# Later rows of x and the map of k: from TensorE transposes to VectorE's 32x32 blocks with quarters moved by DMA, with a newly sought order

## The chip, the cores and the metric

The kernel runs on one core of one Trainium2 chip. The metric is the device time of one execution in microseconds; the kernel before takes 705.9 us, the median of 3 runs (704.93 to 706.68). The profile is of one execution, taken by the hardware profiler.

## The reference

The input is x (2048 rows of 512, float32). It is normalised by rows, and two branches are computed from it and joined:

```
xn = layernorm(x)                                  # rows: (x - mean) / sqrt(var + 1e-5)
q, k, v = xn @ wq, xn @ wk, xn @ wv                # 32 heads of 16
for each of 4 segments s of 512 rows:
    p     = softmax(q_s k_s^T / 4 + causal mask)   # per head
    a_dot = p v_s
    a_mem = (phi(q_s) M) / (phi(q_s) z + 1e-6)     # phi(t) = t + 1 if t > 0 else exp(t)
    o_s   = g a_mem + (1 - g) a_dot                # g = sigmoid(beta) per head
    M += phi(k_s)^T v_s ; z += sum of phi(k_s)
h   = relu(xn @ w1) @ w2                           # 512 -> 1792 -> 512
out = x + (o @ wo) * silu(h)
```

The matmuls have to be more exact than one pass gives, so each operand is split into a high and a low part (xh and xl, wh and wl, and so on), and a product takes three matmuls: high by high, low by high, high by low.

## The kernel before

**Tiling.** The four segments follow one another, 512 rows each. Within a segment the heads are taken in four groups of eight, so there are 16 groups n, and each group has two halves u of four heads. TensorE contracts over the partition axis, so every product that contracts over the 512 columns of x needs x with its columns on partitions: the tiles `xh` and `xl` (128 partitions, 4 column blocks, 512 rows) are the two parts of x turned. They are read by the projections (`proj`, `vproj`) and the first MLP layer (`w1chain`).

**How x is turned before.** `lnload` (L623) loads the four tiles of 128 rows of a segment into buffers of the ring `io`; `lnstat` (L667) takes mean and variance on VectorE (L634), finds 1/sqrt by four Newton steps on GpSimd (L684 to L687), and normalises the tiles in place, two on VectorE and two on GpSimd (L698). `ln` (L709) then turns each tile with four TensorE transposes (L725) into a bank of PSUM, from which ScalarE writes the high part (L732) and VectorE the low one (L733). The first segment has a path of its own, `lnstat0`, in the opening.

**How k is turned before.** For the memory M the product contracts over rows, so phi(k) of a group, tile `pk` (128 head columns on partitions, 512 rows), has to be turned too. `memory` (L1144) does it with four TensorE transposes (L1154) into a bank, which ScalarE copies to `pkT` (L1159). `memory2` (L1166) then multiplies `pkT` by v (L1182). This is done for the 12 groups of the first three segments.

**The rest, where the prediction speaks of it.** Most products run in two lanes, `lanes` (L798): a contraction of 128 is cut into a lower half (L829) and an upper half (L838), each of 64 rows of the array, and the upper half of an earlier product runs beside the lower half of a later one; a half without a partner runs alone. Between them stand the row maxima, q k^T on TensorE (L1225) and a VectorE maximum for each (L1231, `CUSTOM_DVE` in the profile, `ISA` in the order); the scores again for the exponentials (L1277, then L1294 and L1288 on ScalarE); p v (L1323); the memory's numerator and denominator (L1112, L1113). Weights come by DMA into `io` (L516); ScalarE splits off the high part (L527) and GpSimd the low one (L528). q and k go through DRAM (`sdq`, `sdk`, L1064, L1065) to be stacked (L1199), the row maxima too (L1251, L1252). `output` and `silu` (L918, L969, L973) end a segment.

**What sets the order.** Everything is issued by a planner in the kernel's source, class `Sched` (L94): each operation has an assumed length and a due time, and a list scheduler places it on its engine's queue. All DMAs but three go through SyncE's queue, which takes them in order. `search` (L274) repeats the planning twelve times with due times fed back, and then tries random moves, one per number in `STEPS` (L48). The result is one fixed order for every engine. The loop over t in `emit` has 179 steps; group n has its projections at step 10n - 17, `memory(n)` at 10n - 9 and `memory2(n)` at 10n.

## Time and profile before

| | |
|---|---|
| runs | 706.68, 704.93, 705.9 us; median 705.9 |
| span of the profiled execution, first to last instruction | 703.0 us |
| TensorE matmul (PE) / weight load (PEld) | 99% / 79% busy |
| VectorE (DVE), ScalarE (ACT), GpSimd (POOL) | 63%, 59%, 64% busy |
| granted TensorE clock | 1.000 |
| DMA | 125,490 packets, 139.88 MB, 199 GB/s over the span |

The page gives the profiled execution's span alone and no time of its own beside it. Busy shares are means over the whole span. A row of a group reads: line, engine, operation, out<-in, shapes, number | busy us, mean ns of one | idle time before it and what ended that. A piece of the chain that ended last reads: start, length, what. The matmuls on TensorE overlap, so the sum of their lengths is more than the time that they take; the chain's pieces do not overlap. SPq is SyncE's queue of DMA issues.

### The profile page before, as it was taken

How to read it: one execution, taken by the hardware profiler on the slowest of the kernel's cores; microseconds unless marked ns; L12 is line 12 of the kernel's file. 1: busy time of each engine (PE TensorE's matmuls, PEld its weight loads, DVE VectorE, ACT ScalarE, POOL GpSimd, SP SyncE). 2: the span in 40 equal slices, each digit the busy share in tenths (PEclk: the TensorE clock that was granted, in tenths of full speed). 3: DMA queues.
4: the chain of work that ended last, by engine and by line, in shares of the span. 5: the costliest groups of instructions: out<-in, count | busy, mean ns of one | idle time of the engine just before them, and what ended most of it. 6: DMA issues, size and time to landing. Idle time of an engine off the chain costs nothing.

```text
span 703.0 us, 18592 instructions
## 1 busy us (share of the span) xinstructions
PE 696.8 (99%) x6818; PEld 552.8 (79%) x6818; DVE 444.1 (63%) x1398; ACT 413.1 (59%) x633; POOL 448.6 (64%) x567
## 2 busy tenths in 40 slices
PE   8999999999999999999999999999999999999997
PEld 7989787777877688787788878777887977777776
DVE  4357777676968673666683766466577647566427
ACT  5544656666857583475674667446466546665642
POOL 5643754737649476676594947757675667675854
PEclk9999999999999999999999999999999999999999
DMA  5787556656676479475566658837575767763514
GB/s 187 218 271 238 167 173 217 197 171 207 213 256 187 153 245 297 129 232 183 151 218 227 192 169 284 256 118 258 160 245 183 254 200 232 240 220 90 168 22 129
DMA packets 125490, 139.88 MB, mean 199 GB/s; under 512 B 24712, under 2 KB 70024, under 8 KB 125400
## 3 DMA queue, kind: packets, MB, share of 16 engines
q1 hardware_dynamic: 125192, 138.50, 61.7%
q8 instruction: 54, 0.88, 0.5%
q14 instruction: 36, 0.29, 0.1%
q10 hardware_dynamic: 208, 0.20, 0.1%
HBM read 99.01 MB, written 34.93 MB: 191 GB/s over the span
## 4 chain that ended last, share of the span: by engine, by line
PE 97%; DMA 1%; DVE 0%; SPq 0%; issue 0%; ACT 0%; DVEq 0%
PE ps L829 56%; PE ps L838 11%; PE ps L1323 10%; PE pt L1277 6%; PE ps L1225 6%; PE pt L1112 2%; PE ps L725 1%; PE ps L1154 1%; PE ps L789 1%; PE ps L787 1%; PE ps L788 1%; DMA io<-in_A_wv_dram 1%; DMA nn<-F 1%; PE ps L1182 1%; PE pt L787 0%
## 5 line engine op out<-in xcount | busy, mean ns | idle before, releaser
L1231 DVE CUSTOM_DVE_ANT_0 none<-ps,causal 128x256 bf16<-128x256 f32 (+3 forms) x512 | 250.8, 490 | 117.7 <-PE ps L1225 80.2
L528 POOL TENSOR_TENSOR wl<-io,wh 128x512 fp32r<-128x512 f32 x176 | 225.9, 1295 | 77.2 <-ACT wh L527 68.9
L1294 ACT ACTIVATE P<-pt 128x1024 f32<-128x1024 f32 x128 | 131.2, 1025 | 69.5 <-PE pt L1277 66.7
L829 PE MATMUL ps<-xh,wh 64*128 64x512 f32 x352 | 139.5, 396 | 0.0
L838 PE MATMUL ps<-xl,wh 64*128 64x512 f32 x352 | 139.1, 395 | 0.0
L838 PE MATMUL ps<-xh,wl 64*128 64x512 f32 x352 | 136.9, 389 | 0.0
L838 PE MATMUL ps<-xh,wh 64*128 64x512 f32 x352 | 136.8, 389 | 0.0
L829 PE MATMUL ps<-xl,wh 64*128 64x512 f32 x352 | 136.6, 388 | 0.0
L829 PE MATMUL ps<-xh,wl 64*128 64x512 f32 x352 | 136.6, 388 | 0.0
L527 ACT ACTIVATE wh<-io 128x512 fp32r<-128x512 f32 x176 | 108.1, 629 | 25.6 <-PE ps L838 8.7
L1284 POOL TENSOR_SCALAR_AFFINE_SELECT P<-P 128x512 f32<-128x512 f32 x128 | 80.4, 640 | 61.5 <-ACT P L1294 46.4
L838 PE MATMUL ps<-wl,hh 64*128 64x512 f32 x224 | 89.4, 399 | 0.0
L829 PE MATMUL ps<-wh,hh 64*128 64x512 f32 x224 | 89.0, 397 | 0.0
L838 PE MATMUL ps<-wh,hl 64*128 64x512 f32 x224 | 87.2, 389 | 0.0
L838 PE MATMUL ps<-wh,hh 64*128 64x512 f32 x224 | 87.1, 389 | 0.0
L829 PE MATMUL ps<-wh,hl 64*128 64x512 f32 x224 | 86.9, 388 | 0.0
L829 PE MATMUL ps<-wl,hh 64*128 64x512 f32 x224 | 86.9, 388 | 0.0
L1323 PE MATMUL ps<-P,vt 128*17 128x512 f32 (+3 forms) x1024 | 75.1, 434 | 0.0
L829 PEld LDWEIGHTS ps<-xh,wh 64*128 64x128 f32 x352 | 64.9, 185 | 10.5 <-issue 2.8
L829 PEld LDWEIGHTS ps<-xh,wl 64*128 64x128 f32 x352 | 64.8, 184 | 10.4
L1225 PE MATMUL ps<-ks,qs 64*128 64x256 f32 (+3 forms) x512 | 70.4, 324 | 0.3 <-DVE F L1061 0.3
L829 PEld LDWEIGHTS ps<-xl,wh 64*128 64x128 f32 x352 | 65.0, 185 | 6.7
(172 smaller groups left out, 1724.3 us busy)
## 6 DMA issues: line engine op xcount, KB each, us to landing
io<-in_B_w_dram SPq DMA_DIRECT2D x112, 256.0 KB
qs<-sdq SPq DMA_DIRECT2D x32, 512.0 KB
ks<-sdk SPq DMA_DIRECT2D x32, 512.0 KB
sdq<-F SPq DMA_DIRECT2D x16, 512.0 KB
sdk<-F SPq DMA_DIRECT2D x16, 512.0 KB
io<-in_A_x_dram SPq DMA_DIRECT2D x28, 256.0 KB
io<-in_A_wv_dram SPq DMA_DIRECT2D x16, 256.0 KB
io<-in_A_wq_dram SPq DMA_DIRECT2D x16, 256.0 KB
```

The lines of the kernel that those rows point to most:

```text
L527: act(512, [rk], [hk], lambda: ACT.activation(h, raw, AF.Copy), 7.0 + nsplit if early else 6.0)
L528: pool(512, [rk, hk], [lk], lambda: POOL.tensor_tensor(l, raw, r32(h), op=OP.subtract), 8.5 + 1.3 * nsplit if early else 25.4)
L725: PE.transpose(pt[:, 128 * c:128 * c + 128], xt[:, 128 * c:128 * c + 128], ident)
L829: i = PE.matmul(m[0], m[2][0][LO], m[2][1][LO], start=m[4], stop=False)
L838: PE.matmul(h[0], h[2][0][HI], h[2][1][HI], start=False, stop=h[5] is not None)
L1112: PE.matmul(pn[r:r + 64], MZ[r:r + 64, r:r + 64], f[r:r + 64], start=True, stop=True)
L1225: PE.matmul(two[a][0][:, o:o + w], qs[r, p, w - 128:w], ks[r, p, :w], start=True, stop=True)
L1231: dve(w + 40 + TTR, [pk, "causal"], [f"{dk}.{p}{a}{j}"], lambda p=p, j=j, o=o, w=w, a=a, pS=pS: DVE.tensor_tensor_reduce(none[:, :w], pS[: ...
L1277: PE.matmul(pT[:, a, o:o + w], ks[r, p, 128 * i:128 * i + 128], qs[r, p, 128 * i:], start=True, stop=True)
L1284: pool(512, ks, ks, lambda: POOL.affine_select(t, t, pattern=[[0, 4], [1, 128]], compare_op=OP.is_ge, fill=0.0, base=0, channel_multiplier ...
L1294: act(1024, tk, [both[p]], lambda: ACT.activation(P[:, 2 * p:2 * p + 2, :], pT, AF.Exp, scale=0.25), 18.5)
L1323: PE.matmul(pO[32 * b:32 * b + 17, 128 * i:], v, P[:, b, o:o + w], start=i == 0, stop=i == 3)
```

## The change

For the segments after the first, x is loaded a second time, already cut so that VectorE can turn it in blocks of 32 by 32 within its four groups of 32 partitions:

- `lnload` and the statistics stay, but a tile's buffer is given up behind its statistics, and nothing is normalised there. The last Newton step also makes -mean/sigma. The pair (-mean/sigma, 1/sigma) of every row goes to DRAM (`lq`) and comes back spread over partitions, into the first 32 columns of `ident`, which nothing else reads after the first segment (`SQ`).
- `lnagain` loads the tile again with four DMAs of 32 partitions; in each, a partition gets 16 runs of 32 elements (128 bytes), from four rows and four column blocks.
- `lnturn` normalises it with four ScalarE operations of 128 columns, scale and bias per partition, turns all of it with one VectorE block transpose into another buffer of `io`, and splits that: high part on ScalarE, low part on VectorE, now from SBUF and not from PSUM.
- `memory` turns `pk` with one VectorE block transpose, stores it to DRAM (`kd`) and moves the quarters with four loads of 32 partitions each. `memory2` reads `pkT` by its new layout; its matmuls keep their shapes.
- The planner gets prices for the new transfers, caches its look-ups, and can follow a script in part. `STEPS` is a new list of moves, some aimed at a stretch of time or at single operations, and the whole order is sought anew.

The core of the diff:

```diff
-STEPS = (2000081, 2000117, 2000141, 2000147, ...
+STEPS = ((506283, 0, 357.1), (10061542, 3, 568.8), (13857053, 3, 424.9), ...
...
-    "nn": (0.15, 1.00, 1.40), "dq": (0.10, 0.80, 1.20)}
+    "nn": (0.15, 1.00, 1.40), "tr": (0.28, 1.10, 1.70), "sh": (0.42, 1.10, 1.90), "dq": (0.10, 0.80, 1.20)}
...
+            if y2 is not rs:
+                POOL.tensor_tensor(mv[:, :, 0], mv[:, :, 0], y2, op=OP.mult)
+                POOL.tensor_scalar(mv[:, :, 0], mv[:, :, 0], -1.0, None, op0=OP.mult)
...
-        for t in range(4):
-            xt, k = LN[s][t]
-            f = pool if LP and t % 2 else dve
-            f(512, [k, *mks, *rks], [k], lambda xt=xt, t=t: (POOL if LP and t % 2 else DVE).tensor_scalar(
-                xt, xt, mv[:, t, 0:1], rs[:, t:t + 1], op0=OP.subtract, op1=OP.mult), 23.3 + t)
+        d, k = LQR.next()
+        dma(mks, [k], lambda: SP.dma_start(d, mv.rearrange("p t c -> p (t c)")), 12.0, "rq")
+        dma([k], ["sq"], lambda: SP.dma_start(SQ, d.rearrange("(j b) c -> j (b c)", b=4)[None].to_broadcast([4, 32, 32])), 12.0, "rq")
+
+    def lnagain(s, t):
...
+        for a in range(4):
+            dma([k], [ks[a]], lambda a=a: SP.dma_start(
+                xt[32 * a:32 * a + 32].rearrange("j (g i) -> j g i", i=32),
+                x2[s * L + 128 * t:s * L + 128 * t + 128, :].rearrange(
+                    "(j b) (c q i) -> j (b c) q i", b=4, c=KC, q=4)[:, :, a]), 4.0, "sh", also=old)
+
+    def lnturn(s, t):
...
+        for b in range(4):
+            act(128, [*ks, "sq"], [ns[b]], lambda b=b: ACT.activation(
+                xt[:, 128 * b:128 * b + 128], xt[:, 128 * b:128 * b + 128], AF.Identity,
+                scale=sq[:, b, t, 1:2], bias=sq[:, b, t, 0:1]), 6.0)
+        y, yk = IO.next()
+        y4 = y.rearrange("p (c n) -> p c n", c=KC)
+        dve(512, [k, *ks, *ns], [yk], lambda: DVE.transpose(
+            y.rearrange("p (c j b) -> p b c j", c=KC, b=4), xt.rearrange("p (b c i) -> p b c i", b=4, c=KC)), 8.0)
+        IO.held.discard(k)
+        act(512, [yk], [hk], lambda: ACT.activation(hs, y4, AF.Copy), 9.0)
+        dve(512, [yk, hk], [lk], lambda: DVE.tensor_tensor(ls, y4, r32(hs), op=OP.subtract), 10.0)
...
-            for c in range(4):
-                PE.transpose(pt[:, 128 * c:128 * c + 128], pk[:, 128 * c:128 * c + 128], ident)
-
-        S.pe(0.60, fk, [pk_], go)
...
-        act(512, [pk_], [tk], lambda: ACT.activation(pkT.rearrange("p c f -> p (c f)"), pt, AF.Copy), 0.0)
+        d, k = KDR.next()
+        dve(512, fk, tks, lambda: DVE.transpose(
+            pkT.rearrange("p a (t i) -> p a t i", i=32), pk.rearrange("p (t a j) -> p a t j", a=4, j=32)), 2.0)
+        dma(tks, [k], lambda: SP.dma_start(d, pkT.rearrange("p a n -> p (a n)")), 4.0, "put")
+        for a in range(4):
+            dma([k], [tks[a]], lambda a=a: SP.dma_start(
+                pkT[32 * a:32 * a + 32], d[:, 128 * a:128 * a + 128].rearrange("(b j) n -> j b n", b=4)), 4.0, "tr")
```

The order is shown at three places, before and then after. Line numbers after the change are those of the changed file. First TensorE where segment 1's x is turned (before: L1225 row maxima, L725 transposes, L1277 scores, L829 and L838 the two lanes):

```order
L1225 MATMUL ps_117<-ks_84,qs_81 128x512
L725 MATMUL ps_115<-ident,io_121 128x128 x4
L725 MATMUL ps_114<-ident,io_122 128x128 x4
L1277 MATMUL pt<-qs_80,ks_83 128x512 x2
L725 MATMUL ps_116<-ident,io_123 128x128 x4
L725 MATMUL ps_117<-ident,io_124 128x128 x4
L829 MATMUL ps_115<-xh_127,wh_99 128x512
L838 MATMUL ps_113<-xl_129,wh_104 128x512
```

The same row maxima after (L1313 row maxima, L1365 scores, L918 and L927 the lanes):

```order
L1313 MATMUL ps_117<-ks_84,qs_81 128x512
L918 MATMUL ps_116<-xh_127,wh_100 128x512
L927 MATMUL ps_115<-xl_129,wh_99 128x512
L918 MATMUL ps_116<-xl_129,wh_100 128x512
L927 MATMUL ps_115<-xh_127,wl_106 128x512
L918 MATMUL ps_116<-xh_127,wl_107 128x512
L927 MATMUL ps_115<-xh_127,wh_99 128x512
L1365 MATMUL pt<-qs_80,ks_83 128x512 x2
```

The sixteen transposes are gone, and three lane pairs stand between the row maximum and the scores. In the whole order TensorE has 96 transposes fewer, and its lane matmuls without a partner go from 54 to 66.

Second SyncE's queue in front of segment 1's wo product, where segment 2's x is prepared (before: L516 weight loads, L1346 the numerators `nn`, L1199 stacking loads, L1251 row maxima to DRAM):

```order
L1199 DMA ks_83<-sdk_145 128x2x512
L1199 DMA qs_80<-sdq_143 128x2x512
L516 DMA io_123<-in_A_wo_dram 128x512
L1346 DMA nn_177<-F_176 16x512 x7
L516 DMA io_124<-in_A_wo_dram 128x512
L516 DMA io_126<-in_A_wo_dram 128x512
L516 DMA io_125<-in_A_wo_dram 128x512
L1251 DMA mx_167<-mT_165 128x32
```

After (L753 the reloads of x, L743 and L744 the statistics out and back, L1154 a store of k's low part, L1287 stacking loads, L560 weights):

```order
L753 DMA io_121<-in_A_x_dram 32x16x32 x2
L1287 DMA qs_80<-sdq_143 128x2x512
L753 DMA io_121<-in_A_x_dram 32x16x32 x2
L743 DMA lq_156<-mv_194 128x8
L1154 DMA sdk_145<-F_178 128x512
L753 DMA io_122<-in_A_x_dram 32x16x32 x4
L1287 DMA ks_83<-sdk_145 128x2x512
L744 DMA ident<-lq_156 128x1x32
L560 DMA io_125<-in_A_wo_dram 128x512
L753 DMA io_124<-in_A_x_dram 32x16x32 x4
L753 DMA io_120<-in_A_x_dram 32x16x32 x4
L560 DMA io_126<-in_B_w_dram 128x4x128
```

The first of wo's four loads stands just ahead of these rows, the second among them, the other two behind them; two stacking loads and a store now have reloads and the statistics' store in front of them.

Third VectorE in segment 1 (before: L1231 row maxima in two rows each, L733 the low part of x, L1249 a small transpose, L1061 the low part of a projection):

```order
L1231 ISA none,md_160<-ps_117,causal 128x512
L1231 ISA md_160 128x1
L733 TENSOR_TENSOR xl_130<-ps_115,xh_128 128x4x128
L733 TENSOR_TENSOR xl_130<-ps_114,xh_128 128x4x128
L1249 STREAM_TRANSPOSE mT_164<-mm_87 128x32
L733 TENSOR_TENSOR xl_130<-ps_116,xh_128 128x4x128
L733 TENSOR_TENSOR xl_130<-ps_117,xh_128 128x4x128
L1061 TENSOR_TENSOR F_173<-ps_113,F_176 128x512
```

After (L1319 row maxima, L960 the low part of the MLP's hidden layer, L777 the low part of x, L773 the block transposes):

```order
L960 SCALAR_TENSOR_TENSOR hl_142<-ps_114,hh_136 128x512
L777 TENSOR_TENSOR xl_130<-io_120,xh_128 128x4x128
L773 STREAM_TRANSPOSE io_125<-io_126 128x4x128
L773 STREAM_TRANSPOSE io_120<-io_124 128x4x128
L1319 ISA none,md_164<-ps_117,causal 128x512
L1319 ISA md_164 128x1
L1319 ISA none,md_164<-ps_118,causal 128x512
L1319 ISA md_164 128x1
L777 TENSOR_TENSOR xl_130<-io_125,xh_128 128x4x128
```

The low parts stood close together; now they are spread over a longer stretch, with the block transposes between them and row maxima behind these.

More of the change, by code (lines that the diff above doesn't have):

```diff
@@ L110, in __init__ @@
         self.inbank = {}
+        self.found = {}
+        self.waits, self.marks = [], []
         self.owed = Counter()
@@ L153, in op @@
         self.pend[eng].append(o)
+        self.found.pop(eng, None)
         return o
     def start(self, o):
-        return max([o.t, *(t for b in o.banks for n, t in self.inbank.get(b, {}).items() if n != o.eng)])
+        t = o.t
+        for b in o.banks:
+            for n, u in self.inbank.get(b, {}).items():
+                if n != o.eng and u > t:
+                    t = u
+        return t
     def _emit(self, o):
@@ L191, in run @@
             for e in self.ENG:
-                ok = [o for o in self.pend[e] if not o.left]
-                if not ok:
-                    continue
-                f = self.free[e]
-                s = max(f, min(self.start(o) for o in ok))
-                if s < until and (best is None or s < best[0]):
-                    best = (s, ok)
+                got = self.found.get(e)
+                if got is None:
+                    ok = [o for o in self.pend[e] if not o.left]
+                    s = max(self.free[e], min(self.start(o) for o in ok)) if ok else float("inf")
+                    got = self.found[e] = s, ok
+                if got[0] < until and (best is None or got[0] < best[0]):
+                    best = got
             if best is None:
@@ L217, in pe @@
         self.stall += s - self.now
+        if s > self.now:
+            self.waits.append((self.now, s - self.now, max((d for d in deps if d.eng != 'PE'), key=lambda d: d.t)))
         fn()
@@ L281, in fit @@
         for j in range(n):
-            _, got, end, new, _ = run(used, total, e2, taken)
+            _, got, end, new, _, _ = run(used, total, e2, taken)
             if say:
@@ L290, in search @@
     for i in range(PASSES):
-        spent, used, end, new, taken = run(plan, total, ends)
+        spent, used, end, new, taken, _ = run(plan, total, ends)
         if say:
@@ L298, in search @@
     best = min(found, key=lambda f: f[0])
-    for seed in STEPS if seeds is None else seeds(lambda: best[0]):
-        _, plan, total, ends, _ = best
-        rng = Random(seed)
-        move, a, w = rng.choice((0.3, 1.0, 2.0)), rng.uniform(-30.0, 690.0), rng.choice((30.0, 80.0, 800.0))
-        total += rng.choice((0.0, 0.0, rng.gauss(0.0, 1.5)))
-        ends = {k: v + rng.gauss(0.0, move) if a <= v < a + w else v for k, v in ends.items()}
-        spent, used, end, new, taken = run(plan, total, ends)
-        found = []
-        fit(-1, used, taken, ends, total, 1)
-        if found[0][0] < best[0] + 1.5:
-            fit(-1, used, taken, {k: 0.5 * v + 0.5 * ends.get(k, v) for k, v in new.items()}, spent, 2)
-        best = min([best, *found], key=lambda f: f[0])
+    for s in STEPS if seeds is None else seeds(best):
+        best, _ = step(run, best, *s)
     return best
@@ L320, in decide @@
     def decide(f):
-        taken.append(f() if script is None else next(told))
+        got = next(told, None)
+        taken.append(f() if got is None else got)
+        S.marks.append(S.now)
         return taken[-1]
```

111 lines of the change are left out of this document (85 added, 26 removed).

## The prediction

> **What bounds the kernel now.** I read the page first (busy time, then the slices), then the chain of work that ended last, then what TensorE waited for.
>
> ```profile
> span 703.0 us, 18592 instructions
> PE 696.8 (99%) x6818; PEld 552.8 (79%) x6818; DVE 444.1 (63%) x1398; ACT 413.1 (59%) x633; POOL 448.6 (64%) x567
> ...
> PE   8999999999999999999999999999999999999997
> ...
> DMA  5787556656676479475566658837575767763514
> ...
> PE 97%; DMA 1%; DVE 0%; SPq 0%; issue 0%; ACT 0%; DVEq 0%
> ```
>
> TensorE is busy for 99% of the span, in every slice but the ends, and is 97% of the chain; no other engine is over 64%. The answer on its waits has three rows:
>
> ```profile
> PE pt L596 <- POOL epst L395: 1.4, 1, 1.4
> PE ps L725 <- ACT io L656: 0.5, 1, 0.5
> PE ps L1225 <- DVE F L1061: 0.3, 1, 0.3
> ```
>
> They sum to 2.2 us. So after the opening TensorE is never short of work, and what is taken off its list shortens the run by about what it takes there, as long as nothing new arrives late. A newly sought order has next to no waiting to win; it can only lose some.
>
> **The transposes on TensorE.** First the groups by line and form, then pieces of the chain (start, length, what).
>
> ```profile
> L725 PE MATMUL ps<-ident,io 128*128 128x128 f32 x60 | 8.9, 282 | 0.5 <-ACT io L656 0.5
> L1154 PE MATMUL ps<-ident,pk 128*128 128x128 f32 x48 | 7.9, 286 | 0.0
> ```
>
> ```profile
> 1.71 4.20 DMA io<-in_A_wv_dram
> ...
> 100.32 0.59 PE ps L1154 x4
> ...
> 131.65 2.28 PE ps L1323 x32
> ...
> 238.68 0.59 PE ps L725 x4
> ...
> 257.07 1.02 PE ps L725 x8
> ...
> 430.35 1.02 PE ps L725 x8
> ```
>
> ```profile
> 114.41 0.23 PE ps L1225 x2
> 114.65 1.02 PE ps L725 x8
> 115.67 0.42 PE pt L1277 x2
> 116.09 1.02 PE ps L725 x8
> 117.12 0.43 PE ps L829
> ...
> 117.55 0.23 PE ps L829
> ```
>
> Matmuls overlap, so the mean of 282 ns is not the price; the chain's pieces are. Four transposes cost 0.59 us, eight in a row 1.02. The pair of half-height matmuls (L829 with L838) behind them takes 0.43 where the next takes 0.23, so coming back costs 0.20 more.
>
> All 48 of L1154 go: 12 groups x 0.59 = 7.1 us. Of L725 (60 and four more in the opening on pt) the opening keeps 16; the other 48, twelve tiles, go: four pieces of eight and four of four (one of them shown), 4 x 1.02 + 4 x 0.59 = 6.4 us. These 24 groups stand in 20 runs. Returning from a run is worth 0 to 0.20 each, 0 to 4.0; before's order has lane pairs straight behind 11 of them, where the row shows 0.20 (2.2), and I give the other nine half (0.9): 3.1 us. The new order is not quite as well paired: 66 half-height matmuls without a partner against 54, six slots more, at 0.23 each +1.4. TensorE's sum: -7.1 - 6.4 - 3.1 + 1.4 = -15.2 us. The memory product (L1182) takes the same columns from other places of its tile, at no cost.
>
> **What the other engines get.** Means by line; for L918 and the two issues min/median/max.
>
> ```profile
> L733 DVE TENSOR_TENSOR xl<-ps,xh 128x512 fp32r<-128x512 f32 x15 | 10.0, 688 | 2.9 <-ACT xh L732 2.6
> L698 DVE TENSOR_SCALAR io<-io,mv,rs 128x512 f32<-128x512 f32 x6 | 5.5, 908 | 0.0
> L1249 DVE STREAM_TRANSPOSE mT<-mm 128x32 f32<-128x32 f32 x32 | 6.6, 206 | 5.7 <-POOL mm L1240 5.7
> L1187 DVE COPY mc<-ps 128x32 f32<-128x32 f32 x4 | 0.7, 187 | 3.5 <-PE ps L1182 3.5
> L1159 ACT ACTIVATE pkT<-ps 128x512 f32<-128x512 f32 x12 | 7.1, 595 | 3.1 <-PE ps L1154 3.1
> L656 ACT ACTIVATE io<-io,nb,rs 128x512 f32<-128x512 f32 x2 | 1.6, 801 | 0.0
> L1421 ACT ACTIVATE oh<-nn 128x128 fp32r<-128x128 f32 x4 | 1.2, 310 | 5.4 <-POOL nn L1420 5.3
> L527 ACT ACTIVATE wh<-io 128x512 fp32r<-128x512 f32 x176 | 108.1, 629 | 25.6 <-PE ps L838 8.7 <-issue 8.1 <-DMA io<-in_B_w_dram 3.8
> L528 POOL TENSOR_TENSOR wl<-io,wh 128x512 fp32r<-128x512 f32 x176 | 225.9, 1295 | 77.2 <-ACT wh L527 68.9 <-PE ps L1225 2.4 <-DMA ee<-rq 1.9
> ```
>
> ```profile
> L918 DVE SCALAR_TENSOR_TENSOR io<-io,bacc x16: 621/771/1783, 181.7 to 694.1; 128x512 f32<-128x512 f32 x16
> L1252 SPq DMA_DIRECT2D qs<-mx x32: 545/591/697, 61.1 to 658.2; - x32
> L628 SPq DMA_DIRECT2D io<-in_A_x_dram x16: 327/424/466, 0.8 to 376.2; - x16
> ```
>
> VectorE gets 24 block transposes of 512 columns. Only one of 32 columns is on record, 0.206 us, beside a 32-column copy of 0.187. The bounds are 0.21 and sixteen times that, 3.3; I take 0.75, since transpose and copy hardly differ at 32 columns, and 512 columns of other work take 0.69 to 0.77 (L733, L918). 24 x 0.75 = 18 us, less 5.5 (L698), plus about 0.1 for each of 12 subtractions that now read SBUF twice as L918 does: +14, to 458 of 703. ScalarE loses 12 evictions (7.1) and gets 48 normalisations of 128 columns. Bounds 0.31 (L1421) and 0.80 (L656); I take 0.48, L1421 plus the 0.17 by which L656 exceeds L527: +23 - 7 = +16, to 429. GpSimd loses its six normalisations. All of it lies beside TensorE's work and costs nothing unless it is late; without that cover one tile's transpose and subtraction would be 1.5 us of waiting. SyncE issues 48 reloads of x, 6 moves of the statistics and 60 of k, 114 at 0.42 to 0.59, some 57 us more on a queue that is 0% of the chain. The new store of the statistics (L743) waits for GpSimd's last Newton step, and a store of k's lower part, reloads and the next stacking load are queued behind it; the next scores wait for those.
>
> The ring io changes too: a tile of x now leaves its buffer behind its statistics, and takes two others later for a shorter time. A weight load that found none free would come late; I count it with the transfers below.
>
> How late may x be? In segment 1, where it is tightest, TensorE has 42 lane pairs and one product with v between the row-maximum matmuls in front of the last tile's work on VectorE and the first matmul on the new xh: 42 x 0.23 + 2.28 = 12 us. VectorE needs five operations there, about 3.7 us. Some 8 us are left. For k the code puts nine of its 179 steps between `memory` and the product, 9 x 703 / 179 = 35 us; a transpose, five issues and two landings of the longest kind on the chain (4.20) need 0.75 + 3.0 + 8.4 = 12. But ScalarE's order was sought with 0.285 us for a normalisation (the code's formula), 0.2 too little; a group of four then runs 0.8 late. Bounds: nothing, or 0.8 in each of three segments, 2.4; I take 0.8.
>
> A rule that speaks against this part: the Trainium skill, SBUF — State Buffer, Who interferes with whom, says that a VectorE operation with two SBUF inputs and a GpSimd one that reads SBUF shut each other out for a whole instruction. The spread of L918, 0.62 to 1.78, agrees. By that rule a subtraction may wait out a full L528, 1.3 us; if that came on top of the 0.8 once per segment, new waits would be 3 x 2.1 = 6.3 and the time 697.0 instead.
>
> **Sum.** The span goes from 703.0 by -15.2 + 0.8 to 688.6. The page gives no time of that execution beside its span; the median, 705.9, lies 2.9 above it, and opening and tail keep their instructions. 688.6 + 2.9 = 691.5 us.
>
> **Rivals.** The packets of the whole run, then the DMA share (the last but one number) in four stretches:
>
> ```profile
> DMA packets 125490, 139.88 MB, mean 199 GB/s; under 512 B 24712, under 2 KB 70024, under 8 KB 125400
> ...
> q1 hardware_dynamic: 125192, 138.50, 61.7%
> ```
>
> ```profile
> 230.00:235.00 5.00, 5.00 (x48) 3.43 (x46) 3.63 (x13) 2.48 (x5) 2.92 (x5) 1.00 0.63 215
> ...
> 240.00:245.00 5.00, 5.00 (x86) 3.06 (x84) 1.58 (x7) 1.67 (x3) 0.22 (x2) 1.00 0.51 179
> ...
> 260.00:265.00 5.00, 5.00 (x46) 4.29 (x44) 2.68 (x5) 2.02 (x4) 1.97 (x2) 1.00 0.98 351
> 265.00:270.00 5.00, 5.00 (x46) 4.72 (x44) 0.85 (x2) 0.00 (x0) 2.58 (x2) 1.00 1.00 365
> ```
>
> *Transfers become the bound where they are full.* Each segment reloads 1.05 MB in 8,192 runs of 128 bytes. Where wo is used the engines stand at 0.98 to 1.00, so there added work delays weights. (k's four stores and sixteen loads, 2.1 MB a segment, are spread over 170 us or so and left out.) At 351 GB/s x is 3.0 us a segment; at the mean packet (61.7% of 16 x 703 us over 125,192, 55 ns) 28. Three segments at the low end, 9 us: 700.5. For it: the reloads stand close to the loads of wo. Against: in the new order segment 2's are all issued ahead of wo's last two units, at a place where the share was 0.51 to 0.63. The Trainium skill, DMA: Bandwidth & Descriptors, Specifications, asks for 512 bytes or more for full rate; no row here shows the 128-byte runs by themselves. Chance 0.13.
>
> *Slower: block transposes at 3.3 us.* If each block of 32 columns costs what L1249 costs alone, every transpose is 2.6 us longer than I took, with row maxima queued behind it (the order shows two transposes directly ahead of two row maxima). The banks that these empty come free late, and TensorE stands still. 24 x 2.6 = 62; if half comes through, 31: 722. It decides from 0.6 us of stall per transpose (14.4 / 24). Against: 206 beside 187. Chance 0.07.
>
> *No gain: the freed time turns into waiting,* since row maxima, their trip through DRAM and the exponentials follow one another at a pace of their own; then 705.9. Against: TensorE waits for a step of that sequence once, for 0.3 us. Chance 0.06.
>
> **Numbers.** My forecast has 0.74, as 689 to 695. 688.5 is the sum with 4.0 for the returns, no new wait and no unpaired slot (703.0 - 17.5 + 2.9 = 688.4); 700.5 takes in the port rule's 697.0 and the transfers up to their low end. That holds about 0.8. 0.3%, 2 us, is about what can be told from no change. Faster: 0.74 + 0.13 and a sixth of the no-gain case, 0.88; within 0.3%, 0.04; slower, 0.07 and another sixth, 0.08.
>
> **What would show it.** In the profile after: no L1154 group and 16 transposes of x; TensorE still 99%; its waits under 4 us in all; block transposes of 0.7 to 0.8 us; normalisations near 0.48. I am wrong if TensorE waits on xh, pkT or new weights by more than 3 us a segment, or if block transposes are over 1.4 us.

## The result and the profile after

The changed kernel takes 717.36 us (four runs, 712.67 to 719.73); the kernel before took 705.41 beside it. The ratio is 1.0164 (95% interval 1.0138 to 1.0189): slower, where 691.5 and a range up to 700.5 were forecast. The profiled execution took 719.73 us, 1.7 more than its span. Times of kernels are medians; of the seven runs of the kernel without second loads below, two slow ones (744.54 and 3634.76 us) are left out.

From here on line numbers are those of the kernel whose profile is shown. In the changed kernel the half-height lane pairs are L918 with L927 (before L829 with L838), the row maxima L1313 (L1225), the scores again L1365 (L1277), the stacking loads L1287 (L1199). New are the statistics' store L743, x's second loads L753, normalisations L768, block transpose L773 and, for k, the block transpose L1242, the store L1244 and the loads L1246.

From the page of the kernel after: the span, the busy times, TensorE and its clock in slices, the DMA queue, the chain by engine.

```profile
span 718.0 us, 18669 instructions
...
PE 693.9 (97%) x6722; PEld 551.1 (77%) x6722; DVE 459.6 (64%) x1416; ACT 423.8 (59%) x669; POOL 437.8 (61%) x567
...
PE   8999999999999798999899999899999999999997
...
PEclk9999999999999899999999999999999999999999
DMA  5697877776867778466667578865777667863513
...
q1 hardware_dynamic: 160004, 148.01, 67.2%
...
PE 73%; DMA 14%; ACT 4%; DVE 3%; SPq 2%; issue 2%; POOL 1%; DVEq 0%; ACTq 0%; POOLq 0%
```

TensorE has fallen from 97% of the chain to 73%; DMA has gone from 1% to 14%, SyncE's queue from 0% to 2%. TensorE is busy for less than 90% in slices 14, 16, 20, 23 and 29, which begin near 233, 269, 341, 395 and 503 us. What it waited for (us in all, times, longest):

```profile
PE ps L1313 <- DMA ks<-sdk: 6.7, 2, 4.2
PE ps L918 <- ACT wh L571: 4.0, 3, 1.8
PE pt L1365 <- ACT P L1382: 2.7, 5, 0.8
PE ps L918 <- POOL wl L572: 2.5, 3, 0.9
PE pt L640 <- POOL epst L436: 1.4, 1, 1.4
PE ps L814 <- ACT io L700: 1.1, 1, 1.1
PE pt L1365 <- DMA qs<-mx: 0.4, 1, 0.4
PE ps L918 <- DVE mc L1278: 0.4, 1, 0.4
PE ps L918 <- DVE md L1319: 0.2, 1, 0.2
```

The three rows of before summed to 2.2 us; these sum to 19.4. No single releaser carries it: stacking loads, weights that are split late, exponentials that free their banks late. The largest wait, near 242 us, read from the chain (start, length, what):

```profile
236.90 1.22 POOL P L1372 x2
238.12 0.25 SPq L743
...
238.46 0.38 SPq L1154
...
238.89 0.58 SPq L753
...
239.53 0.65 SPq L753
...
240.22 0.62 SPq L753
...
240.89 0.62 SPq L753
...
241.62 5.09 DMA ks<-sdk
...
246.84 0.79 PE ps L1313 x2
```

The statistics' store stands behind GpSimd's work; the store of k's low part, four second loads and then the stacking load stand behind it on SyncE. The stacking load is out 3.5 us after the statistics' store began, and it lands 5.1 us later. In the kernel without second loads, below, no wait for a stacking load is longer than 1.2 us. The prediction described this queue and put no price on it.

A wait also costs more than its length. Stretches around it (PE, PEld, DVE, ACT and POOL busy, then the granted clock, DMA share, GB/s):

```profile
240.00:244.00 4.00, 2.43 (x56) 1.51 (x44) 2.40 (x7) 2.74 (x3) 2.58 (x6) 1.00 0.74 159
244.00:248.00 4.00, 1.16 (x8) 1.13 (x10) 0.36 (x1) 0.49 (x1) 1.70 (x4) 0.59 0.89 213
248.00:252.00 4.00, 4.00 (x26) 3.34 (x26) 3.45 (x11) 3.60 (x7) 0.27 (x1) 0.56 0.69 144
252.00:256.00 4.00, 3.89 (x37) 2.99 (x37) 3.24 (x10) 3.45 (x8) 0.95 (x2) 1.00 0.17 16
```

In 248 to 252 us TensorE is busy throughout and starts 26 matmuls, where a like stretch of the kernel before has 36 to 42: the clock is granted at 0.56. The wait itself is 4.2 us by the row above. Such stretches add up: in the whole profiled execution the clock stood at 0.50 for 17.1 us, in four places, which costs half of that, 8.5 us.

The new work's own durations (ns: min/median/max):

```profile
L753 SPq DMA_DIRECT2D io<-in_A_x_dram x48: 559/625/1413, 77.7 to 436.2; - x48
L768 ACT ACTIVATE io<-io,ident x48: 477/487/498, 101.9 to 443.5; 128x128 f32<-128x128 f32 x48
L773 DVE STREAM_TRANSPOSE io<-io x12: 1076/1110/1185, 105.1 to 444.1; 128x512 f32<-128x512 f32 x12
L1242 DVE STREAM_TRANSPOSE pkT<-pk x12: 669/706/714, 36.7 to 484.7; 128x512 f32<-128x512 f32 x12
```

**Did TensorE lose its 15 us?** To see that beside the waits I priced each stretch of TensorE's order (so many lane pairs, a batch of row maxima, a group of transposes, and what follows what) by what such stretches took in the trace of before, fitted by least squares, and summed the prices over the order of each kernel. Span less that sum is what the kernel waits or runs slowly. By this estimate the changed kernel has 687.9 us of TensorE work, where before has 703.0, and 30.1 us of waiting and slow running. Of the 30.1, 17.2 are the rows of waits above beyond before's 2.2, 8.5 are the slower clock, and some 4 have no name. The prediction's figure for the work alone, 703.0 - 15.2, was 687.8. The same sum is made for every kernel below, always for the one profiled execution, which can lie some us beside the median: 2.4 us above it for the changed kernel.

### The profile page after: what moved, and what is told of

Its sections match the earlier page's. It is cut to its first block, busy times and chain, and to the rows that moved or that the text cites. A ratio compares the mean times of both kernels' runs of the same rounds, so it can differ in the third digit from the quotient of the medians.

```text
span 718.0 us, 18669 instructions
## 1 busy us (share of the span) xinstructions
PE 693.9 (97%) x6722; PEld 551.1 (77%) x6722; DVE 459.6 (64%) x1416; ACT 423.8 (59%) x669; POOL 437.8 (61%) x567
## 4 chain that ended last, share of the span: by engine, by line
PE 73%; DMA 14%; ACT 4%; DVE 3%; SPq 2%; issue 2%; POOL 1%; DVEq 0%; ACTq 0%; POOLq 0%
PE ps L918 41%; PE ps L927 10%; PE ps L1411 8%; PE pt L1365 5%; PE ps L1313 5%; DMA ks<-sdk 3%; DMA io<-in_B_w_dram 2%; DMA sdk<-F 2%; PE pt L1201 1%; DVE none L1319 1%; DMA io<-in_A_wo_dram 1%; DMA mx<-mT 1%; DMA sdq<-F 1%; DVE io L773 1%; ACT P L1382 1%
## 5 line engine op out<-in xcount | busy, mean ns | idle before, releaser
L1319 DVE CUSTOM_DVE_ANT_0 none<-ps,causal 128x384 bf16<-128x384 f32 (+3 forms) x512 | 250.3, 489 | 119.6 <-PE ps L1313 92.1
L927 PE MATMUL ps<-xl,wh 64*128 64x512 f32 x352 | 140.4, 399 | 0.0
L918 PE MATMUL ps<-xh,wh 64*128 64x512 f32 x352 | 139.6, 397 | 0.7 <-DVE mc L1278 0.4
L927 PE MATMUL ps<-xh,wl 64*128 64x512 f32 x352 | 138.2, 393 | 0.0
L918 PE MATMUL ps<-xl,wh 64*128 64x512 f32 x352 | 137.4, 390 | 0.0
L927 PE MATMUL ps<-xh,wh 64*128 64x512 f32 x352 | 137.2, 390 | 0.0
L918 PE MATMUL ps<-xh,wl 64*128 64x512 f32 x352 | 137.1, 389 | 0.0
L918 PE MATMUL ps<-wh,hh 64*128 64x512 f32 x224 | 91.2, 407 | 3.7 <-ACT wh L571 3.5
L927 PE MATMUL ps<-wl,hh 64*128 64x512 f32 x224 | 90.3, 403 | 0.0
L918 PE MATMUL ps<-wl,hh 64*128 64x512 f32 x224 | 88.5, 395 | 1.7 <-POOL wl L572 1.7
L927 PE MATMUL ps<-wh,hh 64*128 64x512 f32 x224 | 88.5, 395 | 0.0
L927 PE MATMUL ps<-wh,hl 64*128 64x512 f32 x224 | 88.2, 394 | 0.0
L918 PE MATMUL ps<-wh,hl 64*128 64x512 f32 x224 | 88.1, 393 | 0.0
L1313 PE MATMUL ps<-ks,qs 64*128 64x256 f32 (+3 forms) x512 | 72.6, 329 | 6.8 <-DMA ks<-sdk 6.7
L1365 PE MATMUL pt<-qs,ks 64*128 64x384 f32 (+3 forms) x512 | 70.5, 323 | 3.2 <-ACT P L1382 2.7
L918 PEld LDWEIGHTS ps<-xh,wl 64*128 64x128 f32 x352 | 65.3, 185 | 9.7
L918 PEld LDWEIGHTS ps<-xh,wh 64*128 64x128 f32 x352 | 65.5, 186 | 8.7 <-issue 1.2
```

What stands on the lines that cost most here:

```text
L918: i = PE.matmul(m[0], m[2][0][LO], m[2][1][LO], start=m[4], stop=False)
L927: PE.matmul(h[0], h[2][0][HI], h[2][1][HI], start=False, stop=h[5] is not None)
L1313: PE.matmul(two[a][0][:, o:o + w], qs[r, p, w - 128:w], ks[r, p, :w], start=True, stop=True)
L1319: dve(w + 40 + TTR, [pk, "causal"], [f"{dk}.{p}{a}{j}"], lambda p=p, j=j, o=o, w=w, a=a, pS=pS: DVE.tensor_tensor_reduce(none[:, :w], pS[: ...
L1365: PE.matmul(pT[:, a, o:o + w], ks[r, p, 128 * i:128 * i + 128], qs[r, p, 128 * i:], start=True, stop=True)
```

## The experiments

Theories, as they stood: Q, the issues on SyncE's in-order queue; E, the time on the transfer engines; V, the longer work on VectorE and ScalarE; O, an order cut so closely that any lateness shows. Each ratio is to the kernel before, which took 704.2 to 705.5 us in all of these comparisons.

**One part taken away, the changed kernel's order kept.** Four kernels.

```diff
-            dma([k], [ks[a]], lambda a=a: SP.dma_start(
-                xt[32 * a:32 * a + 32].rearrange("j (g i) -> j g i", i=32), ...
+            dma([k], [ks[a]], lambda a=a: None, 4.0, "sh", also=old)
```

> The changed kernel in its own order, with the 48 second loads of x (L753) left out: the tiles keep what lay in them, so the normalised x of segments 1 to 3 is not x (the scale is taken from the mean's column to keep it finite). Theory Q (SyncE's in-order queue: 48 issues of 0.63 us, 31 us, stand between the loads that TensorE waits for): the waits at 242, 256 and 282 us go, 12 to 18 of the 30 us of waiting, 699 to 706 us. Theory E (the transfer engines: 48 x 0.42 us of all 16, in 128-byte runs): the same 699 to 706; the next kernel parts the two. Theory V (VectorE and ScalarE: block transposes of 1.11 us and normalisations of 0.49 us hold up the row maxima): nothing, 715 to 720. Theory O (the order itself: every engine's rows are cut so closely that a lateness of any one shows): at most 8 us come back, 709 to 714, and other waits take the places of those that go.

```diff
-                xt[32 * a:32 * a + 32].rearrange("j (g i) -> j g i", i=32),
+                xt[32 * a:32 * a + 32, :32].rearrange("j (g i) -> j g i", i=32),
...
-                    "(j b) (c q i) -> j (b c) q i", b=4, c=KC, q=4)[:, :, a]), 4.0, "sh", also=old)
+                    "(j b) (c q i) -> j (b c) q i", b=4, c=KC, q=4)[:, 0:1, a]), 4.0, "sh", also=old)
```

> The changed kernel in its own order, with each of the 48 second loads cut from 64 KB to 4 KB (one 32-element piece of 16 for each row group; the rest of the tile keeps what lay in it, so x of segments 1 to 3 is not x). The issues stay on SyncE in their places. Theory Q: if the issue time stays near 0.6 us, 714 to 719 us; if it falls with the number of pieces to 0.4 us, 710 to 715. Theory E: the engines get their 19 us back, 699 to 706 as without the loads. Theory V: 715 to 720. Theory O: 709 to 717.

```diff
-        dma(tks, [k], lambda: SP.dma_start(d, pkT.rearrange("p a n -> p (a n)")), 4.0, "put")
+        dma(tks, [k], lambda: None, 4.0, "put")
...
-            dma([k], [tks[a]], lambda a=a: SP.dma_start(pkT[32 * a:32 * a + 32], ...
+            dma([k], [tks[a]], lambda a=a: None, 4.0, "tr")
```

> The changed kernel in its own order, with the 12 stores of the block-transposed k and the 48 loads that move its quarters left out (L1244, L1246): k stays with its quarters in the wrong partitions, so the memory of the segments is wrong. SyncE loses 12 x 0.45 + 48 x 0.49 = 29 us of issues, the engines 12 x 0.8 + 48 x 0.28 = 23 us. Theory Q: the wait at 462 us (a load issued behind the last k move) and its followers go, 5 to 10 us, 707 to 712. Theory E: much the same, 705 to 712. Theory V: 715 to 720. Theory O: 711 to 716.

```diff
-                xt[:, 128 * b:128 * b + 128], xt[:, 128 * b:128 * b + 128], AF.Identity,
+                xt[:, 32 * b:32 * b + 2], xt[:, 32 * b:32 * b + 2], AF.Identity,
...
-            y.rearrange("p (c j b) -> p b c j", c=KC, b=4), xt.rearrange("p (b c i) -> p b c i", b=4, c=KC)), 8.0)
+            y[:, :32], xt[:, :32]), 8.0)
...
-            pkT.rearrange("p a (t i) -> p a t i", i=32), pk.rearrange("p (t a j) -> p a t j", a=4, j=32)), 2.0)
+            pkT.rearrange("p a (t i) -> p a t i", i=32) if n == 0 else pkT[:, 0, :32],
+            pk.rearrange("p (t a j) -> p a t j", a=4, j=32) if n == 0 else pk[:, :32]), 2.0)
```

> The changed kernel in its own order, with the 12 block transposes of x and 11 of the 12 of k cut from 512 to 32 columns and the 48 normalisations from 128 to 2 columns (x of segments 1 to 3 and k are wrong): VectorE loses 12 x 0.9 + 11 x 0.5 = 16 us, ScalarE some 10 us, all transfers stay. Theory V: the waits for row maxima and for the high parts go, 699 to 708 us. Theories Q and E: only the wait at 251 us that a block transpose ends (about 1 us) goes, 714 to 719. Theory O: 712 to 717.

| left out or cut | time, us | ratio (95%) | span | TensorE's work, priced | waits and slow running |
|---|---|---|---|---|---|
| nothing (the changed kernel) | 717.36 | 1.0164 (1.0138 to 1.0189) | 718.0 | 687.9 | 30.1 |
| second loads | 708.01 | 1.0034 (1.0016 to 1.0051) | 706.6 | 687.5 | 19.1 |
| second loads cut to 4 KB | 707.72 | 1.0035 (1.0020 to 1.0050) | 709.1 | 688.1 | 21.0 |
| k's moves | 706.79 | 1.0026 (1.0005 to 1.0047) | 706.2 | 687.9 | 18.3 |
| block transposes and normalisations cut | 712.92 | 1.0089 (1.0055 to 1.0124) | 716.0 | 688.7 | 27.3 |

Each part gives something back, 4 to 11 us, and none gives back most of the 30. Q, E and V each miss as the one cause. The 8 us that O allowed for a single part are passed by 1.4 to 2.6, by the loads and the moves. With the second loads cut to 4 KB two thirds of their issue time stayed (0.419 us of 0.625) and the whole gain came all the same: 707.72 us lies 2.3 us under Q's range and 1.7 over E's. That speaks rather for the transfers' own time in this order, but a third of the issue time went as well, so the pair doesn't part Q from E.

**All moves out, and longer pieces.** Leaving both out:

> The changed kernel in its own order with all 108 added transfers of data left out, the 48 second loads of x and the 12 stores and 48 loads of k (x of segments 1 to 3 and k are wrong). Leaving out the loads of x gave 9 us back of the changed kernel's 717.4 us, leaving out the moves of k 10.6. Theory T (the transfers, their time on the engines and on SyncE's queue, make the waits): the gains add, 696 to 700 us, below the kernel before. Theory O (the order leaves TensorE's needs so close behind what they need that other waits take over): the gains don't add, 703 to 708 us, no faster than before although 96 transposes are gone and no transfer has come.

It took 704.33 us (ratio 0.9981, 0.9966 to 0.9996; span 700.0, priced work 688.1, 11.9 of waits). The two gains, 9.4 and 10.6, come to 13.0 together, not 20: with all 108 transfers gone the order still keeps TensorE waiting, for the split weights among others, as the first row of its waits shows:

```profile
PE ps L915 <- POOL wl L572: 2.3, 3, 1.2
```

That is O's range. The other kernel renumbered the columns, so that a quarter of a row lies in one piece:

```diff
-        src = w[128 * k0:128 * (k0 + kn), c0:c0 + n].rearrange("(k p) f -> p k f", p=128)
+        src = w[128 * k0:128 * (k0 + kn), c0:c0 + n].rearrange("(p k) f -> p k f", p=128)
...
-                    "(j b) (c q i) -> j (b c) q i", b=4, c=KC, q=4)[:, :, a]), 4.0, "sh", also=old)
+                    "(j b) (a f) -> j b a f", b=4, a=4)[:, :, a]), 4.0, "sh", also=old)
```

> The changed kernel in its own order, with the second loads of x in pieces of 512 bytes in place of 128: partition m of chunk c holds feature 4m + c, so that a quarter of a row lies in one piece; the weights' rows, the block transposes' input and segment 0's transposes follow the same numbering, and the result is the reference's. Theory T: the second loads fall from 0.42 us of the engines to about half and from 0.63 us of SyncE to 0.45, the landings of the stacking loads with them, and most of the 9 us that leaving the loads out gave come back, 708 to 712 us. Theory O: 709 to 714 (the fixed order gives back what is last, and the k moves remain). If strided reads cost the block transposes (1.11 us) or segment 0's transposes more, up to 2 us of that are lost again.

It took 719.48 us (1.0199, 1.0180 to 1.0218), over both ranges: nothing gained. The second loads' issue hardly fell, and the w1 loads, whose rows are now taken four neighbours to a partition, take longer to issue than the 0.432 us of the changed kernel:

```profile
L753 SPq DMA_DIRECT2D io<-in_A_x_dram x48: 559/598/1464, 78.9 to 439.8; - x48
...
L560 SPq DMA_DIRECT2D io<-in_B_w_dram x112: 327/569/1867, 10.7 to 668.0; - x112
```

So this is no clean test of the pieces: what it took from the engines it gave to SyncE.

**The order sought anew.** The planner's prices were corrected to the trace and more steps of search were chosen; once for the whole change and once for each half (the other half's functions are those of before), and, as the measure for these, for the kernel before.

```diff
-STEPS = ((506283, 0, 357.1), (10061542, 3, 568.8), ...
+STEPS = (...
...
-        self.now = s + dur
+        self.now = s + dur + (0.4 * min(s - self.now, 4.0) if s > self.now + 0.5 else 0.0)
...
-            act(128, [*ks, "sq"], [ns[b]], lambda b=b: ACT.activation(
+            act(380, [*ks, "sq"], [ns[b]], lambda b=b: ACT.activation(
...
-"stack": (1.60, 1.15, 3.16), ... "sh": (0.42, 1.10, 1.90)
+"stack": (1.60, 1.85, 3.90), ... "sh": (0.50, 1.50, 2.50)
```

> The changed kernel's work in full, its order sought again: the planner is told what the trace showed (x's block transpose 1.11 us in place of 0.68, a normalisation 0.49 in place of 0.285, an issue of the second load 0.67 in place of 0.6, a stacking load's landing 0.7 us later, and that TensorE loses 0.4 us more for each us that it waits), and it is given 52 steps of search that were chosen out of some thousands, in place of 16. Theory O (the order on record is a poor one, the work itself fits): 693 to 702 us, TensorE's waits and slow stretches under 12 us. Theory S (no order of this work keeps TensorE supplied: the transposes' 15 us are paid back in waits by whatever order): 706 to 716, since the planner itself still counts 19 us of waiting in the best order that it found.

> Only k is turned by VectorE and moved by transfers; x is transposed by TensorE as before (48 transposes gone in place of 96, 6.4 of the 15.2 us by the prediction's sum). Order sought with the same prices and a like effort. Theory O: 697 to 702. Theory S: 702 to 709, k's moves alone already cost what its transposes did.

> Only x is turned by VectorE with second loads; k is transposed by TensorE as before (48 transposes gone, about 8 us by the prediction's sum). Order sought with the same prices and a like effort. Theory O: 697 to 702. Theory S: 705 to 714: the second loads and the block transposes meet the other work of the stage around 240 us, where the changed kernel waited most.

> The kernel before in its work (x and k transposed by TensorE), with the order sought by the same new search, 38 steps, the same prices. It shows what the search alone is worth. Theories O and S both: 702 to 707 us, since TensorE had 2.2 us of waits before, and no order can win more than that back. Over 708 would show that the new search or its prices make poorer orders than the old, and then the two resought kernels above are no fair test of the work.

| work, order sought anew | time, us | ratio (95%) | span | TensorE's work, priced | waits and slow running |
|---|---|---|---|---|---|
| the kernel before | 707.61 | 1.0029 (1.0013 to 1.0045) | 706.2 | 704.8 | 1.4 |
| k by VectorE | 707.14 | 1.0025 (0.9999 to 1.0051) | 701.7 | 695.5 | 6.2 |
| x by VectorE | 720.84 | 1.0210 (1.0155 to 1.0264) | 720.9 | 695.2 | 25.7 |
| both | 711.68 | 1.0080 (1.0048 to 1.0112) | 707.1 | 687.5 | 19.6 |

The new prices and search took 5.7 us of the time away (717.36 to 711.68); the order on record was a poor one by about that much. The last column fell by more, from 30.1 to 19.6, because the two profiled executions lie 2.4 us above and 2.9 us below their medians. The 19.6 that stayed are more than the 17.3 that TensorE was spared (704.8 to 687.5): by this search, theory S. The kernel before is 2.3 us slower in its new order than in its own and 0.6 over its range, so the new search is no better than the old.

The halves differ. k alone is even with the kernel before in the same search, as S has it; its profiled execution lies 3.2 us under the median, so its 6.2 us of waits are about 9 at the median, what it spared (9.3). x alone is 13.2 us slower, over the ranges of both theories: its waits grew by 24 us for 9.6 spared. The page of x alone shows three kinds of wait in front, the third behind a normalisation itself:

```profile
PE pt L1366 <- ACT P L1383: 4.3, 4, 3.0
PE ps L918 <- ACT wh L571: 3.1, 1, 3.1
PE ps L1314 <- ACT io L768: 2.5, 1, 2.5
```

All three are ScalarE's work. The search is a matter of luck too: x alone came out 9.2 us slower than both halves together, which hold the same work on x and more. So a difference of that size between two orders says little. Beside k alone the whole change is 4.5 us slower, beside the kernel before x alone 13.2: both say that x's half costs time, not how much.

**Transfers added to the kernel before.** 48 copies that nothing waits for, in before's own order:

```diff
+        def high():
+            ACT.activation(hs, p3, AF.Copy)
+            for q in range(4 if s else 0):
+                SP.dma_start(SCR[16 * s + 4 * t + q - 16].rearrange("j (g i) -> j g i", i=32),
+                             x2[s * L + 128 * t:s * L + 128 * t + 128, :].rearrange(
+                                 "(j b) (c q i) -> j (b c) q i", b=4, c=KC, q=4)[:, :, q])
...
-        act(512, [pk], [f"{hk}.{t}"], lambda: ACT.activation(hs, p3, AF.Copy), 5.0)
+        act(512, [pk], [f"{hk}.{t}"], high, 5.0)
```

> The kernel before, in its own order and with all its work, and beside it 48 copies of 64 KB in 128-byte pieces, issued by SyncE four at a time where a tile of x of segments 1 to 3 has been transposed (they read the rows that the changed kernel's second loads read and write them to a scratch place in memory that nothing reads). Nothing waits for them; they only take 48 issues on SyncE's queue and the engines' time. Theory T (transfers on a chip whose engines are full in stretches make other loads late): the landings of stacking loads and weights stretch, TensorE waits, 710 to 716 us. Theory L (the kernel before has slack for the transfers as such; what fails in the changed kernel is the chain of second load, normalisation, block transpose and subtraction, and the order that fits it in): 705 to 707.

It took 735.17 us (1.0432, 1.0404 to 1.0460), far over both theories: 31 us for transfers without a reader. So the bytes were taken away, and then the queue was changed.

```diff
-                SP.dma_start(SCR[16 * s + 4 * t + q - 16].rearrange("j (g i) -> j g i", i=32),
+                SP.dma_start(SCR[16 * s + 4 * t + q - 16, :, :32].rearrange("j (g i) -> j g i", i=32),
...
-                                 "(j b) (c q i) -> j (b c) q i", b=4, c=KC, q=4)[:, :, q])
+                                 "(j b) (c q i) -> j (b c) q i", b=4, c=KC, q=4)[:, 0:1, q])
```

> The kernel before with the same 48 added copies, each cut from 64 KB to 4 KB (32 pieces of 128 bytes), issued by SyncE in the same places. Theory Q (the issues on SyncE's in-order queue cost: whatever stands behind them starts later): if an issue takes 0.42 us, as in the run with small second loads, 48 x 0.42 = 20 us, 720 to 728 us. Theory E (the engines' time costs): 705 to 710.

```diff
-                SP.dma_start(SCR[16 * s + 4 * t + q - 16].rearrange("j (g i) -> j g i", i=32),
+                ACT.dma_start(SCR[16 * s + 4 * t + q - 16].rearrange("j (g i) -> j g i", i=32),
```

> The kernel before with the same 48 added copies of 64 KB, issued by ScalarE in place of SyncE, behind the activation that ends a tile's transposes. SyncE's queue is as in the kernel before; ScalarE (59% busy) has 48 issues more. Theory Q: 706 to 714, the rest of it ScalarE's own lateness. Theory E: 728 to 737, as from SyncE.

The issues of the three kernels, one fence each (large from SyncE, small from SyncE, large from ScalarE; ns min/median/max, first and last start):

```profile
L736 SPq DMA_DIRECT2D scr<-in_A_x_dram x48: 490/624/2400, 114.8 to 462.6; - x48
```

```profile
L736 SPq DMA_DIRECT2D scr<-in_A_x_dram x48: 488/588/2187, 115.0 to 458.2; - x48
```

```profile
L736 ACTq DMA_DIRECT2D scr<-in_A_x_dram x48: 497/552/1083, 114.9 to 459.2; - x48
```

With a sixteenth of the bytes the issue keeps its 0.59 us, and the time is 732.00 (1.0376, 1.0355 to 1.0398), above Q's range: 3 of the 31 us belong to the engines' time, some 27 to the issues. That this is near the 48 x 0.588 = 28 us that they last is partly chance: TensorE's waits grew by 17 us, and behind them the clock stood at 0.50 for 17 us, which cost another 8.5. From ScalarE's queue the time is 733.53 (1.0396, 1.0369 to 1.0422), inside E's range and no better. There the copies hold up ScalarE, and the exponentials are what TensorE waits for first:

```profile
PE pt L1285 <- ACT P L1302: 7.8, 2, 4.4
PE ps L1233 <- DVE xl L741: 5.0, 1, 5.0
```

E is out as the main cause for the copies from SyncE, since the small ones cost nearly as much. Q is right that issues cost, but another queue did not help. The kernel with ScalarE is not a test of the issues alone, though: the profile puts the end of some 26 us of ScalarE's idle time down to the copies' landings, so there something did wait for them.

**What it is in x.** The last three have orders of their own. First the whole change without second loads (the tile stays where it lies):

```diff
-            IO.held.discard(k)
...
-        xt, k = IO.next(True)
-        LN[s][t] = xt, k
...
-        y, yk = IO.next()
+        y, yk = FR.next(); yks = [f"{yk}.0", f"{yk}.1"]
```

> Both halves of the change, with x's second loads gone: a tile of x stays where the first load put it until it is turned (so its quarters lie wrongly and x of segments 1 to 3 is not x), and the turned tile goes through one of the four F tiles in place of an io tile, since the held ones leave none. Everything else, the four normalisations and the block transpose too, as in the changed kernel; order sought anew with the corrected prices, 46 steps. If the second loads are what keeps TensorE waiting, 694 to 700 us. If it is the longer way of a tile and the tiles that it holds, 708 to 716, no better than the 711.7 us of the resought order with the loads; the planner itself counts 21 us of waiting in this order.

Then, from there, with the work cut as well:

```diff
-            act(380, [*ks, "sq"], [ns[b]], lambda b=b: ACT.activation(
-                xt[:, 128 * b:128 * b + 128], xt[:, 128 * b:128 * b + 128], AF.Identity,
+            act(1, [*ks, "sq"], [ns[b]], lambda b=b: ACT.activation(
+                xt[:, 32 * b:32 * b + 2], xt[:, 32 * b:32 * b + 2], AF.Identity,
...
-        dve(512, [k, *ks, *ns], yks, lambda: DVE.transpose(
-            y.rearrange("p (c j b) -> p b c j", c=KC, b=4), xt.rearrange("p (b c i) -> p b c i", b=4, c=KC)), 8.0, 1.9e-3)
+        dve(64, [k, *ks, *ns], yks, lambda: DVE.transpose(
+            y[:, :32], xt[:, :32]), 8.0)
```

> As x_held (both halves, no second loads, the tile held, the turned tile in an F tile), with the 48 normalisations cut to 2 columns and x's 12 block transposes to 32 columns, the high part scaled to stay finite and the low part made of the high part alone (x of segments 1 to 3 is not x); order sought anew, 43 steps, with prices to match. If the work of VectorE and ScalarE on x's way is what holds TensorE up, 696 to 703 us. If it is the order of the steps, the held tiles or k's half that does, 709 to 716, like the 716.6 us of x_held; the planner itself counts 12.5 us of waiting, against 21 for x_held.

And, apart from these, k's half with the planner's old prices:

> The k half alone (x transposed by TensorE), order sought with the planner's old prices, 34 steps; by the planner's count it ends 0.2 us after the kernel before. If the k half is worth what its transposes cost less 3 us of waits, 700 to 704 us, and it beats the kernel before; if the saved 9.6 us of TensorE's time go into waits again, 705 to 709.

Without the second loads: 716.58 us (1.0157, 1.0121 to 1.0192), 22.5 us of waits and slow running, 4.9 us slower than the resought order with the loads. So taking the loads away did not close the order. But this kernel also holds its tiles longer and takes F tiles from other work, and 4.9 us is within the search's luck, so it doesn't show that the loads are free. With the work cut too: 699.75 us (0.9921, 0.9891 to 0.9950), 10.4. The rows of the latter's normalisation and block transpose, against 482 and 1100 ns in the former:

```profile
L768 ACT ACTIVATE io<-io,ident x48: 370/377/407, 103.0 to 428.2; 128x2 f32<-128x2 f32 x48
```

```profile
L773 DVE STREAM_TRANSPOSE F<-io x12: 197/211/213, 104.2 to 428.3; 128x32 f32<-128x32 f32 x12
```

48 x 0.105 us of ScalarE and 12 x 0.89 of VectorE, 5 and 11 us, were taken away and 16.8 us of time went. The low part no longer waits for the transpose there either, so it isn't those durations alone; and by the search's luck some us of the 16.8 may be the order's. The k half with old prices took 704.53 us (0.9993, 0.9974 to 1.0013; priced work 694.7, waits 8.2), between its two ranges: the same as before. No kernel that does the whole computation beat the kernel before.

## Why the prediction was wrong

**TensorE's sum was right,** as far as the priced orders can tell: -7.1, -6.4, -3.1 and +1.4 made -15.2, and they give -15.1. "What is taken off its list shortens the run by about what it takes there" held for the list, and "as long as nothing new arrives late" is where it broke.

**The step that failed is the allowance for new waits,** "Bounds: nothing, or 0.8 in each of three segments, 2.4; I take 0.8". The profile has 30.1 us of waits and slow running in its place: 17.2 of waits beyond before's, 8.5 of a slower clock, for which the sum had no term at all, and some 4 without a name. The forecast had the warning sentence itself ("it can only lose some") and gave the loss almost nothing. Three things went into the 0.8:

- *SyncE's 114 issues "on a queue that is 0% of the chain".* A share of the chain says that the queue is not late now, not that it has room. 48 issues of 0.59 us that carry almost no bytes cost the kernel before 27 us. In the changed kernel the planner knows of its issues and places them, and they cost less: leaving all the moves out gave 13 us. But the wait at 242 us is the queue that the prediction described.
- *The slack of the new chains,* 8 us for x and 23 for k, was counted from the tile that is turned to its reader. The readers of that tile were not the ones to wait: no row of TensorE's waits names xh, xl or pkT. Others were, the stacking loads, the weights' split, the exponentials, which stand on the same in-order queues as the new work; the wait at 242 us shows one of them behind it. That count needs to be made for them.
- *Sizes.* A normalisation takes 0.487 us (forecast 0.48); k's block transpose 0.706 (0.75); x's 1.110, not 0.75, which is 4.3 us more of VectorE. That ScalarE's order was sought with 0.285 for a normalisation was seen, but its cost was taken as 0.8 us in all. With the prices put right and more search 5.7 us of the time went, so wrong durations in the plan and too short a search cost about that; the two were not parted.

**The rivals.** *No gain: the freed time turns into waiting* had 0.06 and was nearest. What spoke against it, that TensorE waits once for 0.3 us, was read from an order made for the old work. It could not name a loss, because it let the waits grow only to the time freed; with the transposes gone the resought order waits 19.6 us for 17.3 spared. *Transfers where they are full* had the place wrong: the largest wait stands where the share was 0.74 and 0.89, and in before's order the copies' bytes were a tenth of their cost (3 of 31 us). A packet of 128 bytes took 13 ns in the changed kernel, so a segment's 8,192 runs take 16 engines 6.7 us, near the low end of 3 and far from 28. *The price of a subtraction that waits out a GpSimd operation*, behind the 697.0, came in part: five of the twelve subtractions of L777 took 0.98 to 1.80 us where the median is 0.70, 3.6 us more in all, but no row of TensorE's waits names one. *Block transposes at 3.3 us* didn't occur. The case on the slower side should have been late queues, and much likelier than 0.08.

**What is shown and what is not.** Shown: that waits and a slower clock stand in the place of what TensorE was spared (about 15 us by the priced orders), that the transfers (13 us in that order) and the order (5.7 us) each carry part of it, and that x's half costs time while k's is even. Likely, but not shown: that in x it is the work on ScalarE and VectorE rather than the second loads, since the kernels that say so differ in more than that, and each has an order of its own. Open: whether a better search would find an order of the whole change without waits (the planner's own count for the best one found with these prices still had 19 us of waiting), and how the 5.7 us divide between prices and search. Larger rings for the tiles were not tried.

## What to carry to other kernels

When one engine is busy for 99% under an order sought for it, work moved to other engines is free only if the order can be closed again: ask what stands behind each new instruction on its in-order queue and who waits for that, not how late the new result itself may be. Test the room before the change: a few dozen issues of small copies at the place where the new ones will stand tell what a queue can bear, here 27 us for 48. Count the slower clock behind a wait together with the wait. And compare profiled executions by their distance from the median before comparing their waits: here that distance was up to 3 us, and the two orders of the whole change looked 10.5 us apart in their waits where their times were 5.7 apart.

## What the runs showed of the hardware

The clock drops in steps of 3.41 us, and the length of the wait alone does not decide it. In the changed kernel it stood at 0.50 from 244.7 to 251.5 us, and for 3.41 us from 285.7, 343.7 and 466.6 us; these starts lie 41.0, 58.0 and 122.9 us apart, whole multiples of 3.413. The waits there were 4.2 us, 1.6 and 0.8, 2.5, and 1.8 and 0.9. In the resought order a wait of 1.35 us at 422 us brought 3.41 us of 0.50, and one of 2.1 us at 281 us none. There TensorE is also short of work where the changed kernel waited most, in waits of 1.0 and 1.4 us, and the clock stays at 1.00:

```profile
244.00:248.00 4.00, 2.13 (x58) 1.18 (x46) 2.81 (x7) 4.00 (x8) 0.37 (x1) 1.00 1.13 309
248.00:252.00 4.00, 3.30 (x27) 2.28 (x27) 3.42 (x11) 3.71 (x7) 3.48 (x7) 1.00 0.51 81
```

The Trainium skill, TensorE: Matmul & The Clock Gate, Part 1: The HAM clock gate, says that about 3.4 us without work bring the array's clock to half and as long a busy stretch brings it back. The traces agree in the length of the step and not in the rest: in the changed kernel the clock fell 2.0 us into the wait of 4.2 us and was back 4.7 us behind its end.

An issue's length follows the access pattern more than the bytes: 0.625 us for 512 pieces of 128 bytes, 0.598 for 128 pieces of 512, 0.419 for 32 of 128, yet 0.588 for these 32 when they go from memory to memory. A block transpose of 512 columns takes 0.706 us where the turned rows are written contiguously and 1.110 where they are written at every fourth element. And a normalisation of two columns takes 0.377 us where one of 128 takes 0.487: most of it does not depend on the size, so the four pieces in which a tile is normalised cost 1.95 us where one of 512 columns took 0.80 in the kernel before (L656).
